# A shorter row of work ahead of the first FFN step, and matmuls on constants in TensorE's idle time there

## The chip, the core and the metric

The kernel runs on one core of a Trainium2 chip. A core has five engines with a queue each, worked off in order: TensorE (PE, matmuls into PSUM), VectorE (DVE), ScalarE (ACT), GpSimd (POOL) and SyncE (SP, which here issues all DMA transfers). They wait for one another by semaphores. The metric is the device time of one execution in microseconds (us).

## What is computed

Windowed attention with global tokens, then a block of a Fourier transform and an FFN, for 8 batches of 544 rows of 512 numbers, all in float32:

```python
s_g  = scale * q_g @ k_all.T;  out_g = softmax(s_g) @ v_all
s_ll = where(|i - j| <= 32, scale * q_l @ k_l.T, -1e9)
s_lg = scale * q_l @ k_g.T
out_l = softmax(concat(s_lg, s_ll)) @ concat(v_g, v_l)
x = concat(out_g, out_l)                    # heads side by side, (8, 544, 512)
mixed = real(fft(fft(x, axis=1), axis=2))
u  = x + mixed
un = (u - mean(u)) / sqrt(var(u) + 1e-6)
out = u + relu(un @ w_ch1) @ w_ch2          # 512 -> 2048 -> 512
```

The weights come as 64-bit numbers. Products in TensorE are made of float16 halves: each operand is split into a high and a low half, and three of the four products are summed (high x high, high x low, low x high).

## The kernel before

**Work and loops.** All work is cut into jobs, a method each of the class `Kern`. A planner (`Plan`, Python that runs when the kernel is built) holds for each job its engine, a cost, what it reads and writes, and a due time; it places them one after another, on each engine the ready job with the earliest due time, and `emit` writes them out in that order. So constants at the head of the file (due times such as `W2_AT`, costs, which tile a step uses) decide the order on every engine. The chip then follows that order, whatever its own durations.

**Stages.** Weights: 32 pieces are loaded (`w_load`), put together from their 64-bit words (`w_low` on POOL or ACT, `w_split64` on ACT into one of two PSUM tiles `ps1`, `w_size` L409 and `w_sign` L423 on DVE), summed on PE (`w_sum` L419), and split: the high half on ACT (`w_hi`), the low half in `w_lo`, on DVE as one instruction (L452), or on POOL as two (L449, L450) for the eight pieces listed in `LOP`. Attention: batch by batch, four pairs of heads each, four units of 128 rows a pair: scores on PE (L604), mask and maximum on DVE (`masked`, L612), exponents and high half on ACT, low half on POOL (`p_lo`, L628), a transposing DMA (`turn`, L633), values on PE (`values`, L649 and L652), division on DVE (`norm`, L663 to L665). Around the rows of the global tokens two rows are swapped by a pair of small DMAs (`x_mid`, L743 and L744). DFT of a batch: even and odd parts on DVE (`d_odd` partly on POOL; `d_even` L812 to L818, `d_even2`, `d_odd2`), halves (`d_hi`, `d_lo` L847), the first DFT on PE (`d_first`, five steps L893 and L895, read out by ACT in `d_z` and DVE in `d_z2` L913), the second DFT (`d_second` L928), added onto the rows by DVE (`d_addc` L954, `d_add` L945); a small rest in `d_tailsec`. FFN: 17 chunks of 256 rows. A chunk has its layer norm on DVE (`l_bn` to `l_v`, then `l_un` L1007, the normalized row in float32, `l_hi` its high half on ACT, `l_lo` L1015 its low half on DVE), a transposing DMA per 128 rows (`l_turn`), and eight times a first step (`f_first` L1047, 24 matmuls of 128x256) and a second step (`f_second` L1066, 12 of 128x512, into the two PSUM tiles `acc0` and `acc1`), with ReLU and halves between them on ACT and DVE (L1052, L1056); at the end DVE reads out the sums (`f_end` L1071).

**Order around the change.** Attention of batch 0 and all weight pieces come first, then the DFT of batch 0, then the layer norm of chunk 0, then the first `f_first`. From there on FFN steps fill PE, and attention and DFT of the next batches are placed between them. PSUM: four general tiles (`bk`, given out as they fall free), two `ps1` and `acc0`, `acc1`. `SPARE` names those PSUM tiles which the DFT of batch 0 may use besides, since no FFN runs yet.

Of the kernel before, what the change touches and what calls it, by code (L numbers as in the profile page):

```python
# [7 lines left out]
F32 = mybir.dt.float32  # L8
F32R = mybir.dt.float32r
F16 = mybir.dt.float16  # L10
# [10 lines left out]
P = 128  # L21
# [9 lines left out]
T0 = 130.0  # L31
STEP = 5.25
PERIOD = 109.0
U_AT, U_PACE = 9.0, 4.0
B_AT, B_PACE = 150.0, 5.0
W_AT, W_PACE = 7.0, 2.6
W2_AT, W2_PACE = 48.0, 2.6
S_AT, S_PACE = 25.0, 4.2
S2_AT, S2_PACE = 190.0, 5.0
B_HOLD = 0.0  # L40
# [1 line left out]
PEF = 1.65  # L42
PEM, PEM0, SPM = 1.5, 0.6, 0.2
LOOK = {"ACT": 0.5, "DVE": 0.5, "POOL": 0.8, "SP": 0.5}
ALOW = 4
LOP = (1, 3, 5, 7, 9, 11, 13, 15)
EARLY = 6
L_HOLD = 50.0
QUEUE = 4.0
LOOK_BY = 30.0  # L50
LN, LN1, LN2 = 50.0, 30.0, 40.0
LNB = True
SPARE = {0: "acc0", 1: "acc1", 4: "ps1", 2: "ps1", (0, 0): "acc0", (0, 1): "acc1"}
BLOCK = (0, 3, 1, 2)


# [65 lines left out]
class Plan:  # L122
# [165 lines left out]
            todo -= 1  # L288

    def emit(self):  # L290
        for j in self.order:
            j.fn(*j.a)


class Kern:
# [524 lines left out]
    def d_even2(self, b):  # L820
# [4 lines left out]
        ve.tensor_add(v(f, 0, 129), c[:, :, 0:129], c[:, :, 256:127:-1])  # L825
        ve.tensor_sub(v(f, 258, 128), c[:, :, 0:128], c[:, :, 256:128:-1])

    def d_odd2(self, b):
        se, s4 = self.nc.vector, self.D[b]["s4"]
        self.odd_rows(se, s4[:, :, P:2 * P])  # L830
        c = s4[:, 2:4, 1:256]
        f = s4[:, 0:2].rearrange("p a d -> p (a d)")
        v = lambda t, o, n: t[:, o:o + 2 * n].rearrange("p (k d) -> p k d", k=2)
        se.tensor_sub(v(f, 0, 128), c[:, :, 0:128], c[:, :, 254:126:-1])
        se.tensor_add(v(f, 256, 128), c[:, :, 0:128], c[:, :, 254:126:-1])
# [166 lines left out]

    def l_un(self, c, j):
        L = self.L[c]
        L["un", j] = un = self.p1.tile([P, DM], F32, name="un", tag="un")
        L["hl", j] = hl = self.p2.tile([P, 2, DM], F16, name="unh")
        self.nc.vector.tensor_scalar(un, self.u_row(c, j), L["ve"][:, 1, j:j + 1], L["ve"][:, 2, j:j + 1], op0=ALU.mult, op1=ALU.add)  # L1007

    def l_hi(self, c, j):
        L = self.L[c]  # L1010
        self.nc.scalar.activation(L["hl", j][:, 0], L["un", j], AF.Copy)

    def l_lo(self, c, j):
        L = self.L[c]
# [70 lines left out]
    def jobs_weights(self, add):  # L1085
# [22 lines left out]
        for m in range(32):  # L1108
            k, t = divmod(m, 16)
            i = t if k else 4 * (t % 4) + t // 4  # L1110
            j = i % 4 * 4 + i // 4 if k == 0 else (i + 16) % 18
            w = (f"w{j}", "w", m)
            h = (f"a{i}" if k == 0 else f"w{(i + 14) % 18}", "h", m)
            self.whobj[k, i] = h
            T = S_AT + S_PACE * m if k == 0 else S2_AT + S2_PACE * t
            ws = ("ws", 0, t // 4) if k == 0 else ("ws", 1, 3)
            add("ACT", .63, self.w_hi, k, i, r=[w, ws], w=[h], t=T)
            if m in LOP:
                add("POOL", 1.95, self.w_lo, k, i, True, r=[w], w=[h], t=T + 1)
            else:  # L1120
                add("DVE", 1.15, self.w_lo, k, i, False, r=[w], w=[h], t=T + 1)

    def jobs_batch(self, add, b):
        gn = ("gn", b)
# [99 lines left out]
            add("POOL", 1.26, self.g_fix, g, r=[("xtg", g), *both("xA")], w=both("xA") + [("xtf", g)], k=[X, xt])  # L1224

    def jobs_dft(self, add, b):
        rate, pem = (PEF, PEM0) if b == 0 else (1.0, PEM)
        accx, dsc, e4, xt, s4, X = ("accx", b), ("dsc", b), ("e4", b), ("xt", b), ("s4", b), ("X", b)
        xtg = [(n, 2 * b + i) for n in ("xtm", "xtf") for i in range(2)]
        add("ACT", .40, self.g_square, b, r=[("xgo", b, 0), ("xgo", b, 1)], w=[accx], k=[("xg", b)])  # L1230
# [8 lines left out]
            add(eng, us, self.d_odd, b, i, r=src, w=[s4h[i]] + ([] if i else [s4]), k=[X, s4])  # L1239
            add("DVE", 3.0 if i else 2.9, self.d_even, b, i, r=src, w=[x4h[i]] + own, k=[X, e4])  # L1240
        add("DVE", 1.35, self.d_even2, b, r=x4h, w=x4h, k=[e4])
        add("DVE", 2.3, self.d_odd2, b, r=s4h, w=s4h, k=[s4], late=6.0)
        et, ht = ("et", b), ("ht", b)
        add("POOL", 3.85, self.d_tail, b, r=xtg, w=[et, ("un", "st", b)], k=[xt])
        eh = [("eh0", b), ("eh1", b)]
# [31 lines left out]
    def jobs_chunk(self, add, c):  # L1277
# [7 lines left out]
            add("DVE", .88, self.l_bn, c, j, r=r0[j:j + 1], w=[("mv", c)], k=[X], t=L, back=LNB)  # L1285
        add("DVE", .80, self.l_v, c, r=[("mv", c)], w=[ve], t=L, back=LNB)
        for j in range(2):
            un, hl = ("un", c, j), ("unh", c, j)
            add("DVE", .58, self.l_un, c, j, r=r0[j:j + 1] + [ve], w=[un, hl], k=[X], t=L, back=LNB)
            add("ACT", .55, self.l_hi, c, j, r=[un], w=[hl], t=L, back=LNB)  # L1290
            add("DVE", .70, self.l_lo, c, j, r=[un, hl], w=[hl], t=L, back=LNB)
            add("SP", 1.3, self.l_turn, c, j, r=[hl], c=[uh], svc=1.6, t=L, margin=SPM, back=LNB)
        add("POOL", 3.0, self.l_root, c, r=[ve, ("ws", 1, 3)], w=[ve], t=T, back=False)
# [21 lines left out]
    def make_plan(self):  # L1315
        one = ["e4", "gn", "xg", "pg", "pgr", "s4", "et", "ht", "eh0", "eh1", "z0", "z1", "zr",
               "un", "lw", "asm", "acc0", "acc1"] + [f"w{i}" for i in range(18)] + [f"a{i}" for i in range(16)]
        rings = dict.fromkeys(one, 1)
        rings.update(qk=3, vf=4, kT=2, qT=2, vN=2, vB=2, gT=2, plg=1, pe=4, ph=3, pl=3, X=3, uh=2, unh=2, ve=4, mv=2, ps1=2,
                     acc=2, accx=2,  dsc=2, z=3, nm=4, ng=2, h=3, ge=2, ra=2, rb=2, es=2, xt=2)  # L1320
        plan = self.plan = Plan(rings, {"bank": 4})
        self.whobj = {}
        add = plan.add
        add("SP", .41, self.msk_load, w=[("msk",)], svc=.7, t=U_AT - 8)
        add("SP", 1.8, self.load_consts, w=[("const",)], svc=2.5, t=U_AT + 20)
        self.jobs_weights(add)
        for b in range(B):
            self.jobs_batch(add, b)
            for p in range(4 * b, 4 * b + 4):
                self.jobs_pair(add, p)  # L1330
            self.jobs_dft(add, b)
        for c in range(17):
            self.jobs_chunk(add, c)
        plan.targets(1.3)
        plan.run()

# [53 lines left out]
```

## Time and profile before

| what | us |
|---|---|
| median of three timed runs | 1033.93 (1028.98 to 1034.74) |
| the profiled execution | 1033.84 |
| its span, first to last instruction | 1032.1 |
| first instruction of the first `f_first` | 146.53 |
| end of the last FFN step | 1022.30 |

The profile is one execution, measured by the chip's profiler. A row of the timeline gives the start, the duration, the engine, the line, the operation, what it writes and reads, and in brackets how long the engine stood idle before it and what ended that. A row of a table by stretches gives the bounds of the stretch, its length, the busy time of each engine with its number of instructions, the clock that TensorE was granted (1.00 is full speed), the busy share of the DMA engines and GB/s. In a list of groups the columns are busy time, mean ns of one, and idle time before them with what ended it; in a list of waits: us in total, times, longest.

### The profile page before, as it was taken

How to read it: one execution, taken by the hardware profiler on the slowest of the kernel's cores; microseconds unless marked ns; L12 is line 12 of the kernel's file. 1: busy time of each engine (PE TensorE's matmuls, PEld its weight loads, DVE VectorE, ACT ScalarE, POOL GpSimd, SP SyncE). 2: the span in 40 equal slices, each digit the busy share in tenths (PEclk: the TensorE clock that was granted, in tenths of full speed). 3: DMA queues.
4: the chain of work that ended last, by engine and by line, in shares of the span. 5: the costliest groups of instructions: out<-in, count | busy, mean ns of one | idle time of the engine just before them, and what ended most of it. 6: DMA issues, size and time to landing. Idle time of an engine off the chain costs nothing. (4 is left out here: it accounts for less than half of the span.)

```text
span 1032.1 us, 25192 instructions
## 1 busy us (share of the span) xinstructions
PE 929.6 (90%) x9864; PEld 651.0 (63%) x9864; DVE 658.1 (64%) x1773; ACT 589.4 (57%) x1291; POOL 531.8 (52%) x797
## 2 busy tenths in 40 slices
PE   2354459999999999999999999999999999999996
PEld 1243347767677767676766676777767676666673
DVE  4887999977768855785598568856775456311111
ACT  7996769973677477637863876487436332111110
POOL 7999756862687278626863774486437302000000
PEclk9985569999999999999999999999999999999998
DMA  9898356462685287328752864466225402102000
GB/s 364 254 269 238 105 107 138 106 140 42 141 130 133 45 160 154 77 55 147 134 131 53 132 155 96 88 117 140 39 55 102 83 1 64 42 1 41 2 21 21
DMA packets 221359, 111.52 MB, mean 108 GB/s; under 512 B 196376, under 2 KB 203704, under 8 KB 221240
## 3 DMA queue, kind: packets, MB, share of 16 engines
q1 hardware_dynamic: 221240, 109.91, 48.5%
q8 instruction: 77, 1.26, 0.5%
q14 instruction: 42, 0.34, 0.1%
HBM read 47.37 MB, written 9.44 MB: 55 GB/s over the span
## 5 line engine op out<-in xcount | busy, mean ns | idle before, releaser
L1047 PE MATMUL ps<-uh,wh 128*128 128x256 f16 x3264 | 379.7, 274 | 0.9 <-DMA uh<-unh 0.9
L1066 PE MATMUL acc<-wh,h 128*128 128x512 f16 x1632 | 375.2, 380 | 1.5 <-DVE h L1056 1.0
L1047 PEld LDWEIGHTS <-wh 128*128 128x128 f16 x3264 | 316.1, 98 | 51.2 <-issue 2.0
L1066 PEld LDWEIGHTS <-h 128*128 128x128 f16 x1632 | 154.3, 98 | 170.3 <-issue 2.5
L1056 DVE SCALAR_TENSOR_TENSOR h<-ps,h 128x512 f16<-128x512 f32 x136 | 93.6, 689 | 236.2 <-ACT h L1052 236.0
L1052 ACT ACTIVATE h<-ps 128x512 f16<-128x512 f32 x136 | 80.7, 593 | 256.4 <-PE ps L1047 255.8
L628 POOL TENSOR_TENSOR ph<-pe,ph 128x448 f16<-128x448 f32 (+1 forms) x128 | 139.4, 1103 | 79.3 <-ACT ph L623 63.3
L612 DVE CUSTOM_DVE_ANT_0 pe<-bk,msk,z 128x224 f32<-128x224 f32 (+1 forms) x256 | 102.4, 454 | 17.4 <-PE bk L604 14.2
L619 ACT ACTIVATE pe<-pe,nm 128x224 f32<-128x224 f32 (+1 forms) x256 | 104.7, 476 | 14.2 <-DVE nm L612 13.9
L1027 POOL TENSOR_TENSOR ve<-ve 128x2 f32<-128x2 f32 x17 | 3.9, 230 | 179.8 <-DVE un L1007 179.8
L649 PE MATMUL bk<-vN,pl 128*128 128x65 f16 x768 | 67.4, 201 | 26.6 <-DMA pl<-ph 17.9
L623 ACT ACTIVATE ph<-pe 128x448 f16<-128x448 f32 (+1 forms) x128 | 71.0, 579 | 22.0 <-DMA pl<-ph 15.2
L649 PEld LDWEIGHTS <-pl 128*128 128x128 f16 x768 | 59.5, 103 | 28.8 <-DMA pl<-ph 23.5
L652 PEld LDWEIGHTS <-pl 96*128 96x128 f16 (+1 forms) x768 | 57.5, 103 | 10.0 <-issue 5.9
L604 PE MATMUL bk<-kT,qT 64*128 64x192 f16 (+2 forms) x1536 | 57.5, 221 | 6.5 <-POOL kT L588 4.2
L604 PEld LDWEIGHTS <-qT 64*128 64x128 f16 x1536 | 50.1, 99 | 20.8 <-issue 16.7
L652 PE MATMUL bk<-vB,pl 96*128 96x65 f16 (+1 forms) x576 | 51.5, 202 | 0.0
L563 POOL TENSOR_TENSOR vN<-vf,vN 128x640 f16<-128x640 f32 x32 | 45.8, 1431 | 6.8 <-ACT vN L559 6.6
L419 PE MATMUL wl<-wm,partb 128*128 128x256 bf16 x64 | 18.8, 398 | 32.0 <-DVE wm L409 32.0
L588 POOL TENSOR_TENSOR kT<-qk,kT 128x559 f16<-128x559 f32 x32 | 40.7, 1271 | 11.8 <-ACT kT L583 11.6
L573 ACT ACTIVATE qk<-qk,z 128x559 f32<-128x559 f32 x64 | 43.7, 729 | 2.1 <-DVE z L514 2.0
L508 ACT ACTIVATE junk<-qk 128x512 f16<-128x512 f32 x64 | 41.3, 645 | 4.4 <-DMA qk<-in_qk 3.4
(170 smaller groups left out, 1350.0 us busy)
## 6 DMA issues: line engine op xcount, KB each, us to landing
qk<-in_qk SPq DMA_DIRECT2D x32, 535.5 KB, 5.2
rw<-in_moe_w_ch SPq DMA_DIRECT2D x22, 512.0 KB, 5.2
vf<-in_v SPq DMA_DIRECT2D x32, 320.0 KB, 3.3
out<-X SPq DMA_DIRECT2D x16, 512.0 KB, 3.1
raw<-in_moe_w_ch SPq DMA_DIRECT2D x10, 512.0 KB
vB<-vN SPq DMA_DIRECT2D x32, 97.5 KB, 2.2
vB<-vN SPq DMA_DIRECT2D x64, 32.5 KB, 2.0
pl<-ph SPq DMA_TRANSPOSE x128, 3.2
```

What stands on the lines that cost most here:

```text
L563: self.nc.gpsimd.tensor_sub(vN[:, :, 1, :, 0:64], self.st[p]["vf"], vN[:, :, 0, :, 0:64])
L604: nc.tensor.matmul(S[h][:, t + w0:t + w1], qT[r, a, j], kT[r, k0:k0 + w1 - w0], start=m == 0, stop=m == 2)
L612: nc.vector.tensor_tensor_reduce(self.per[j][:, h, 0:w], S[h][:, t:t + w], self.msk[:, j, 0:w], z[:, 8:9], 3e38, op0=ALU.add, op1=ALU.min, ...
L619: self.nc.scalar.activation(pe[:, h], pe[:, h], AF.Exp, bias=nm[:, h:h + 1], scale=-1.0)
L623: self.nc.scalar.activation(ph[:, 0, :, 0:WIDE[i % 4]], self.per[i % 4][:, :, 0:WIDE[i % 4]], AF.Copy)
L628: self.nc.gpsimd.tensor_sub(ph[:, 1, :, 0:w], self.per[i % 4][:, :, 0:w], ph[:, 0, :, 0:w])
L649: nc.tensor.matmul(pv[:, j % 2, h], pl[:, 4 * a + 2 * h], vN[:, j, c, h, :], start=m == 0, stop=False)
L652: nc.tensor.matmul(pv[:, j % 2, h], pl[0:n, 4 * a + 2 * h + 1], vb, start=False, stop=m == 2)
L1047: nc.tensor.matmul(ps[:, q], wt[:, w, c0:c0 + P], uh[:, :, 4 * a + kt, :], start=n == 0, stop=n == 11)
L1052: self.nc.scalar.activation(h[:, 0], self.fps[c, fp], AF.Relu)
L1056: self.nc.vector.scalar_tensor_tensor(h[:, 1], self.fps.pop((c, fp)), 0.0, h[:, 0], op0=ALU.max, op1=ALU.subtract)
L1066: nc.tensor.matmul(self.acc_f[c][j], h[:, a, q, j * P:(j + 1) * P], self.w[1, f][:, w, :], start=f == 0 and a == 0 and w == 0, stop=f == 1 ...
```

## The change

It has four parts.

1. Constants of the planner: due times of units and of the second weights, all low halves of weights on DVE (`LOP` empty), cheaper planner costs for two steps, and other PSUM tiles for the DFT of batch 0 (first-DFT steps 0 and 1 now in the two `ps1` tiles).
2. `d_odd2` is split in two jobs, so that the even low half can stand between them.
3. Layer norm: the high half is made by ACT straight from the row (scale and bias of the row as operands) instead of from the float32 row; the second float32 row of a chunk has a buffer of its own (that of `lw`); the high half no longer waits for the float32 row.
4. `warm`: a matmul of 128x512 on two constant tables, into a general PSUM tile that nobody reads. 84 of them are given to the planner, with the lowest urgency and not before planner times 104 and 110; those that it places behind the first `f_first` are not written out, and 56 remain.

```diff
-U_AT, U_PACE = 9.0, 4.0
+U_AT, U_PACE = 4.0, 4.0
-W2_AT, W2_PACE = 48.0, 2.6
+W2_AT, W2_PACE = 40.0, 2.6
-LOP = (1, 3, 5, 7, 9, 11, 13, 15)
-EARLY = 6
+LOP = ()
+EARLY = 4
+WARM = ((14, .45, 104.0), (70, .27, 110.0))
-SPARE = {0: "acc0", 1: "acc1", 4: "ps1", 2: "ps1", (0, 0): "acc0", (0, 1): "acc1"}
+SPARE = {0: "ps1", 1: "ps1", 4: "acc0", (0, 0): "acc0", (0, 1): "acc1"}
...
     def emit(self):
+        t0 = min(j.start for j in self.order if j.fn.__name__ == "f_first")
         for j in self.order:
+            if j.fn.__name__ == "warm" and j.start > t0:
+                continue
             j.fn(*j.a)
...
+    def d_odd1(self, b):
+        self.odd_rows(self.nc.vector, self.D[b]["s4"][:, :, P:2 * P])
     def d_odd2(self, b):
         se, s4 = self.nc.vector, self.D[b]["s4"]
-        self.odd_rows(se, s4[:, :, P:2 * P])
...
     def l_un(self, c, j):
-        L["un", j] = un = self.p1.tile([P, DM], F32, name="un", tag="un")
-        L["hl", j] = hl = self.p2.tile([P, 2, DM], F16, name="unh")
+        L["un", j] = un = self.p1.tile([P, DM], F32, name="un", tag=("un", "lw")[j])
     def l_hi(self, c, j):
-        self.nc.scalar.activation(L["hl", j][:, 0], L["un", j], AF.Copy)
+        L["hl", j] = hl = self.p2.tile([P, 2, DM], F16, name="unh")
+        ve = L["ve"]
+        self.nc.scalar.activation(hl[:, 0], self.u_row(c, j), AF.Identity, scale=ve[:, 1, j:j + 1], bias=ve[:, 2, j:j + 1])
...
-                add("DVE", 1.15, self.w_lo, k, i, False, r=[w], w=[h], t=T + 1)
+                add("DVE", .85, self.w_lo, k, i, False, r=[w], w=[h], t=T + 1)
+    def warm(self, n):
+        self.nc.tensor.matmul(self.bank(("bank", "wm", n)), self.c1[:, 0, 0, 0:P], self.c2.rearrange("p a b c d -> p (a b c d)")[:, 0:512], start=True, stop=True)
+    def jobs_warm(self, add):
+        n = 0
+        for count, us, hold in WARM:
+            for _ in range(count):
+                add("PE", us, self.warm, n, r=[("const",)], w=[("bank", "wm", n)], t=1e6, hold=hold, margin=.1)
+                n += 1
...
-        rate, pem = (PEF, PEM0) if b == 0 else (1.0, PEM)
+        rate, pem = (1.1, PEM0) if b == 0 else (1.0, PEM)
...
-        add("DVE", 2.3, self.d_odd2, b, r=s4h, w=s4h, k=[s4], late=6.0)
+        add("DVE", 1.3, self.d_odd1, b, r=s4h[1:], w=s4h[1:], k=[s4], late=4.0)
+        add("DVE", .95, self.d_odd2, b, r=s4h, w=s4h, k=[s4], late=5.0)
...
-            un, hl = ("un", c, j), ("unh", c, j)
-            add("DVE", .58, self.l_un, c, j, r=r0[j:j + 1] + [ve], w=[un, hl], k=[X], t=L, back=LNB)
-            add("ACT", .55, self.l_hi, c, j, r=[un], w=[hl], t=L, back=LNB)
+            un, hl = (("un", "lw")[j], c, j), ("unh", c, j)
+            add("ACT", .60, self.l_hi, c, j, r=r0[j:j + 1] + [ve], w=[hl], k=[X], t=L, back=LNB)
+            add("DVE", .58, self.l_un, c, j, r=r0[j:j + 1] + [ve], w=[un], k=[X], t=L, back=LNB)
```

The change moves instructions on every engine. Lines shift with it: a line of the kernel before has a number higher by 4 to 7 in the changed kernel (L612 becomes L616, L1007 becomes L1012, L1047 becomes L1054).

**DVE, from the read-out of the first DFT to the layer norm of chunk 0.** L913 (L919 in the change) reads out a first-DFT step, L612 (L616) is half of a masked score unit with its small companion. Before:

```order
L913 SCALAR_TENSOR_TENSOR z_1621<-dps,z_1621 128x2x144
L612 ISA pe_81,nm<-bk_129,msk,z 128x224
L612 ISA nm 128x1
L612 ISA pe_81,nm<-bk_131,msk,z 128x224
L612 ISA nm 128x1
L913 SCALAR_TENSOR_TENSOR z_1621<-dps,z_1621 128x2x144
L913 SCALAR_TENSOR_TENSOR zr<-dps,zr 1x2x144
L913 SCALAR_TENSOR_TENSOR z_1660<-dps,z_1660 128x2x144
L612 ISA pe_82,nm<-bk_130,msk,z 128x224
L612 ISA nm 128x1
L612 ISA pe_82,nm<-bk_128,msk,z 128x224
L612 ISA nm 128x1
```

And the same place now (a row that ends in x2 stands for two like it):

```order
L919 SCALAR_TENSOR_TENSOR z_1595<-dps,z_1595 128x2x144 x2
L919 SCALAR_TENSOR_TENSOR zr<-dps,zr 1x2x144
L919 SCALAR_TENSOR_TENSOR z_1626<-bk_130,z_1626 128x2x144
L919 SCALAR_TENSOR_TENSOR z_1626<-bk_129,z_1626 128x2x144
L616 ISA pe_80,nm<-bk_131,msk,z 128x256
L616 ISA nm 128x1
L616 ISA pe_80,nm<-bk_128,msk,z 128x256
L616 ISA nm 128x1
```

The read-outs now stand in one row, and one masked unit instead of three stands ahead of the second DFT's read-out. A little further on, at the end of the layer norm of chunk 0, before (L517 to L537 are scales of the next pair, L954 the read-out of the second chunk):

```order
L1007 TENSOR_SCALAR un<-X,ve 128x512
L517 TENSOR_SCALAR z<-z 128x2x2
L535 SCALAR_TENSOR_TENSOR z<-z 128x2
L536 TENSOR_SCALAR z<-z,ge 128x2
L537 TENSOR_SCALAR z<-z 128x2x2
L1015 TENSOR_TENSOR unh<-un,unh 128x512
L1007 TENSOR_SCALAR un<-X,ve 128x512
L954 SCALAR_TENSOR_TENSOR X<-bk_129,dsc,X 128x2x128 x4
L1015 TENSOR_TENSOR unh<-un,unh 128x512
```

And now, to the read-out of the second chunk (L960, L951):

```order
L1012 TENSOR_SCALAR un<-X,ve 128x512 x2
L1022 TENSOR_TENSOR unh<-un,unh 128x512 x2
L616 ISA pe_81,nm<-bk_131,msk,z 128x224
L616 ISA nm 128x1
L616 ISA pe_81,nm<-bk_128,msk,z 128x224
L616 ISA nm 128x1
L960 SCALAR_TENSOR_TENSOR X<-bk_130,dsc,X 128x2x128 x4
L951 SCALAR_TENSOR_TENSOR X<-bk_129,dsc,X 128x2x128 x4
```

The four pieces of the layer norm follow one another; the scales and the second chunk's read-out come after them.

**PE, ahead of the first FFN step.** `wh` is a weight's halves, `uh` the transposed halves of the layer norm, `c1r` and `c2r` are constant tables of the DFT. Before, the DFT's tail stands directly ahead of the step:

```order
L928 LDWEIGHTS z_1660
L928 MATMUL bk_131<-c2r,z_1660 32x129
L928 LDWEIGHTS z_1660
L928 MATMUL bk_131<-c2r,z_1660 32x129
L1047 LDWEIGHTS wh
L1047 MATMUL ps_1859<-uh,wh 128x256
```

And now, the last four of 21 fillers (L1131) that stand between the second DFT and the step:

```order
L1131 MATMUL bk_128<-c2r,c1r 128x512
L1131 LDWEIGHTS c1r
L1131 MATMUL bk_130<-c2r,c1r 128x512
L1131 LDWEIGHTS c1r
L1131 MATMUL bk_129<-c2r,c1r 128x512
L1054 LDWEIGHTS wh
L1054 MATMUL ps_1812<-uh,wh 128x256
```

The DFT's tail, the values of units 16 and 17, half of a unit's scores and a small total stand behind the first FFN step now. The other 35 fillers stand ahead of the first DFT or within it (33), and between its second-DFT steps (2). The first of the 21 writes `bk_128`, which one masked unit (17) reads.

**SP, around the row swaps of batch 1.** L743 and L744 (L747 and L748) are the pair of `x_mid`, L633 (L637) the transposes for the values of the next pairs, L567 to L464 loads of the next batch, L1077 (L1084) an output. Before:

```order
L743 DMA X<-xt 1x16x16
L744 DMA xt<-xd 1x16x16
L567 DMA vB_66<-vN 64x780
L568 DMA vB_66<-vN 32x2x260
L569 DMA vB_66<-vN 64x260
L495 DMA vf_68<-in_v 128x640
L464 DMA gn<-in_g 128x256
L633 DMA_TRANSPOSE pl<-ph 128x8x128 x3
```

And now:

```order
L747 DMA X<-xt 1x16x16
L748 DMA xt<-xd 1x16x16
L1084 DMA out<-X 128x2x512
L495 DMA qk<-in_qk 128x1071
L571 DMA vB_66<-vN 64x780
L572 DMA vB_66<-vN 32x2x260
L573 DMA vB_66<-vN 64x260
L499 DMA vf_68<-in_v 128x640
L495 DMA qk<-in_qk 128x1071
L468 DMA gn<-in_g 128x256
```

Four more transfers (the second half of `vB` and `vf_69`) follow there, and only then the transposes: twelve transfers stand between the pair and them, where there were five.

More of the change, by code (lines that the diff above doesn't have):

```diff
@@ L1333, in make_plan @@
             self.jobs_chunk(add, c)
+        self.jobs_warm(add)
         plan.targets(1.3)
```

## The prediction

> **What bounds the kernel now.** The page comes first, then stretches of the run, then the instructions at the ends of those stretches.
>
> ```profile
> span 1032.1 us, 25192 instructions
> PE 929.6 (90%) x9864; PEld 651.0 (63%) x9864; DVE 658.1 (64%) x1773; ACT 589.4 (57%) x1291; POOL 531.8 (52%) x797
> PE   2354459999999999999999999999999999999996
> ```
>
> TensorE (PE) is full from the seventh of 40 slices on. So the time is two things laid end to end: the head before the first FFN step, where PE mostly waits, and the PE work that is left after it. The view of busy time by stretches, cut at the events of the head, says who is busy in each:
>
> ```profile
> core 0: us, PE busy (x) PEld busy (x) DVE busy (x) ACT busy (x) POOL busy (x), PEclk, DMA share, GB/s
> 13.75:110.00 96.25, 45.81 (x595) 30.95 (x595) 77.77 (x208) 83.39 (x177) 87.38 (x97) 0.79 0.95 266
> 110.00:142.50 32.50, 11.68 (x131) 8.85 (x131) 31.54 (x77) 25.76 (x57) 23.71 (x31) 0.61 0.40 97
> 142.50:146.50 4.00, 2.43 (x31) 1.77 (x28) 3.83 (x11) 0.48 (x1) 3.09 (x11) 0.50 0.81 104
> 146.50:152.08 5.58, 5.55 (x30) 3.80 (x32) 4.41 (x13) 2.75 (x6) 2.25 (x6) 0.50 0.30 60
> 152.08:1022.30 870.22, 863.69 (x9087) 605.12 (x9081) 538.65 (x1457) 470.00 (x1036) 407.30 (x635) 1.00 0.44 88
> ```
>
> Row 1 is attention of batch 0 together with the weight preparation: GpSimd (POOL) is busy 87.38 of 96.25 us, the most of any engine, and the DMA engines 0.95. Row 2 is the DFT and layer norm of batch 0: VectorE (DVE) is busy 31.54 of 32.50 us, so the chain there is simply DVE's row of instructions. Row 3 is the last transposing DMA. Row 4 is the first FFN step at clock 0.50. Row 5 is PE alone: 863.69 of 870.22 us. The ends of these stretches, in the timeline:
>
> ```profile
> 111.39 0.68 DVE L812 TENSOR_TENSOR e<-X 128x512 f32<-128x512 f32 x1
> 141.83 0.68 DVE L1015 TENSOR_TENSOR unh<-un,unh 128x512 f16<-128x512 f32 x1
> 146.53 3.79 PE L1047 MATMUL ps<-uh,wh 128*128 128x256 f16 x17 [0.92 <-DMA uh<-unh]
> ```
>
> The second even part of the DFT starts at 111.39, the last low half of the layer norm ends at 142.51 (31.1 us later), and the first FFN step starts at 146.53, released by its DMA. Any move of these three points moves the end by as much, as long as PE stays full behind them.
>
> **Term A, attention of batch 0.** Eight low halves of weights leave POOL for DVE. Instructions of the stretch to 110 us, grouped by line (the last numbers are idle time before them), DVE's first piece there, and whom the DMA queue (SP) waited for with its transposes in 25 to 105 us:
>
> ```profile
> L449 POOL TENSOR_SCALAR wm<-wm,wsc 128x512 f32<-128x512 f32 x8 | 13.4, 1673 | 0.5
> L450 POOL TENSOR_TENSOR wh<-wm,wh 128x512 f16<-128x512 f32 x8 | 9.7, 1210 | 0.7
> L452 DVE SCALAR_TENSOR_TENSOR wh<-wm,wsc,wh 128x512 f16<-128x512 f32 x8 | 6.8, 844 | 0.0
> L409 DVE SCALAR_TENSOR_TENSOR wm<-ps,lw 128x512 int32<-128x512 int32 x32 | 21.8, 686 | 23.6 <-ACT ps L396 17.8 <-POOL lw L405 5.7
> 13.75 0.69 DVE L409 SCALAR_TENSOR_TENSOR wm<-ps,lw 128x512 int32<-128x512 int32 x1 [11.66 <-ACT ps L396]
> SPq L633 <- POOL lw L405: 11.8, 5, 4.4
> SPq L633 <- POOL ph L628: 5.5, 3, 2.9
> ```
>
> POOL loses 13.4 + 9.7 = 23.1 us, DVE gains eight more of the third row, 6.8 us. Two of DVE's weight signs (0.6 us each) also leave the stretch, see B. Then POOL has 64.3 us, ACT 83.4, DVE 77.8 + 6.8 - 1.2 = 83.4. If the new fullest engines reach the occupancy that POOL reached, 87.38 / 96.25 = 0.91, the stretch takes 83.4 / 0.91 = 91.6 us: 4.6 us less. The bounds are 0, because the DMA share of 0.95 leaves no room if transfers are what binds, and -8, about half of SP's 17.3 us of waits for POOL, since a transfer that is issued earlier still meets the same queue. I take **-3.5**: ACT and DVE would both be near the limit, which is worse than one.
>
> **Term B, DFT to layer norm.** DVE is packed here, so the chain changes by what is taken out of its row and put in. Out: two of the three masked score units (L612, four instructions each), the scales of the next pair, and the cosine part of the second chunk (L954, four instructions), all now behind the last low half:
>
> ```profile
> 128.70 0.44 DVE L612 CUSTOM_DVE_ANT_0 pe<-bk,msk,z 128x224 f32<-128x224 f32 x1
> 129.44 0.48 DVE L913 SCALAR_TENSOR_TENSOR z<-dps,z 128x288 f16<-128x288 f32 x1
> 138.30 0.16 DVE L517 TENSOR_SCALAR z<-z 128x4 int32<-128x4 int32 x1
> 139.07 0.69 DVE L1015 TENSOR_TENSOR unh<-un,unh 128x512 f16<-128x512 f32 x1
> 140.26 1.65 DVE L954 SCALAR_TENSOR_TENSOR X<-bk,dsc,X 128x256 f32<-128x256 f32 x4
> 110.79 0.68 DVE L423 SCALAR_TENSOR_TENSOR wm<-ps,wm 128x512 int32<-128x512 int32 x1
> 125.18:128.02 2.84, 2.84 (x22) 2.37 (x23) 2.70 (x10) 2.48 (x8) 1.05 (x1) 0.50 0.28 113
> ```
>
> One masked unit takes 129.44 - 128.70 = 0.74, two 1.5; the scales 139.07 - 138.30 = 0.8; L954 1.65: together 3.95 us out. In: two weight signs (L423, ended at 111.39) that stood ahead of the DFT now stand between its halves, 1.2 us. That is -2.75. What fills the place of the masked units is then a wait: a first-DFT step is 8 matmuls, which at half clock take 2.84 / 22 x 8 = 1.0 us (last row, a stretch of these steps), and the evacuations of the five now follow one another with nothing between. Two steps stand behind the last low half of the DFT; one runs beside the weight maximum, so I charge one, 1.0 us, bounds 0 (full clock) and 2. **-1.7.** The layer norm's new pairing (high half straight from the row on ACT, both float rows on DVE) is not charged apart: DVE's row holds the same four instructions, and ACT's high half runs beside the second float row, 0.55 us.
>
> **Term C, fillers and clock.** After the last DFT matmuls PE is idle, and 21 fillers (128x512) stand directly ahead of the first FFN step. The first of them writes a bank that masked unit 17 reads, and that unit is the DVE piece right behind the last low half, so they start about 0.9 us after it. The price of a filler at full clock is that of an FFN matmul of the same shape, from the chain of waits; the clock comes from half-microsecond stretches:
>
> ```profile
> 1017.09 5.19 PE acc L1066 x24
> 133.71 0.51 PE L928 MATMUL bk<-c2r,z 128*128 128x129 f16 x6 [0.77 <-DVE z L514]
> 125.18 0.30 PE L893 MATMUL dps<-c1r,eh 128*128 128x144 f16 x1 [4.07 <-DVE eh L847]
> 128.00:128.50 0.50, 0.50 (x8) 0.48 (x8) 0.50 (x5) 0.38 (x2) 0.00 (x0) 0.82 0.00 0
> 135.00:135.50 0.50, 0.00 (x0) 0.00 (x0) 0.50 (x2) 0.50 (x2) 0.50 (x1) 0.51 1.17 243
> 152.00:152.50 0.50, 0.50 (x20) 0.49 (x18) 0.02 (x1) 0.45 (x1) 0.36 (x2) 0.92 1.11 215
> ```
>
> 5.19 / 24 = 0.216 us at full clock, so 0.43 at half. The clock rose at 128.18 (0.82 is 0.32 us of full speed in that half microsecond), 3.0 us after PE became busy at 125.18; it fell at 135.0, 0.8 us after PE stopped at 134.2; it rose at 152.08, 5.6 us after 146.53. So a rise takes 3.0 to 5.6 us of work; I take 4.4. In the change PE is idle some 8 us ahead of the fillers, as it is now, so they begin at half clock: 4.4 / 0.43 = 10 at half, 11 at 0.216 = 2.4 us, 6.8 in all, and the first FFN step starts 0.9 + 6.8 = 7.7 us after the last low half, where it is 4.0 now. That costs 3.7. Saved is the first step's half clock, now (152.08 - 146.53) / 2 = 2.8. **+0.9**, bounds -0.5 (rise after 3.0) and +1.7 (after 5.6, and one more wait on a bank). The fillers are therefore not ahead of idle time alone; they end behind the DMA that they cover. The 33 fillers ahead of the first DFT cost nothing: what follows them waits for DVE.
>
> The three clock edges lie 6.82 = 2 x 3.41 and 17.07 = 5 x 3.41 us apart. [...]
>
> **Term D, PE work that moves behind the first FFN step.** One score half, two value steps, the DFT's tail and a small total ran in the head. The last three of these in the head, by a stretch, and a score half at full clock:
>
> ```profile
> 141.90:145.70 3.80, 2.96 (x37) 2.30 (x36) 3.70 (x10) 0.43 (x2) 3.08 (x11) 0.50 1.01 134
> 217.24 0.82 PE L604 MATMUL bk<-kT,qT 64*128 64x192 f16 x24
> 220.63 0.24 PE L649 MATMUL bk<-vN,pl 128*128 128x65 f16 x1 [2.57 <-DMA pl<-ph]
> ```
>
> 2.96 at half clock is 1.5 at full; with 0.8 for the scores **+2.3**. Their cover, PE's idle time, is gone once PE is full, so all of it counts.
>
> **Term E, waits behind the first FFN step.** Row 5 of the stretches has 6.5 us of idle PE. The longest piece is the last row above, 2.57 us for a transposed block, and the clock falls with it:
>
> ```profile
> 209.85 0.69 SPq L743 DMA_DIRECT2D X<-xt  x1
> 212.34 0.51 SPq L744 DMA_DIRECT2D xt<-xd  x1
> 220.00:220.50 0.50, 0.00 (x0) 0.00 (x0) 0.00 (x0) 0.00 (x0) 0.50 (x1) 0.84 1.08 211
> 223.50:224.00 0.50, 0.50 (x3) 0.15 (x2) 0.50 (x1) 0.48 (x1) 0.50 (x2) 0.74 0.22 43
> 1021.09 0.75 DVE L1071 SCALAR_TENSOR_TENSOR X<-acc,ve,X 128x512 f32<-128x512 f32 x1 [2.64 <-PE acc L1066]
> ```
>
> From 220.34 to 223.76 (the 0.84 and the 0.74 of the two clock rows) PE ran at half clock: 1.6 us of its 3.1 busy us there lost, 4.2 us with the wait. The cause stands on SP: the pair of row swaps of batch 1 (L743, then L744, which waits 2.5 us for the first), and behind it, after five loads, the transposes of the next batch. In the change's order twelve transfers stand between the same pair and those transposes, and the value steps they serve come behind later FFN steps. So this wait should go; but only one FFN first step of 2.6 us then stands between the last second step of chunk 0 and the first of chunk 1, and that one waits until two pieces of 0.75 us (last row) have read the sums out, behind whatever DVE has in hand: I charge 1.7. Bounds -4.2 and +1; **-2.5**.
>
> **The sum.** The profiled execution took 1033.84 us (its span and 1.7 around it), the median of the three timed runs is 1033.93, the same for this purpose. 1033.84 - 3.5 - 1.7 + 0.9 + 2.3 - 2.5 = **1029.3 us**.
>
> **Rivals.**
> 1. Transfers bind the attention stretch. For it: DMA share 0.95. Against: SP's 17.3 us of waits for POOL are times in which nothing was issued. A is 0 and the time 1032.8.
> 2. Slower: DVE becomes the bound between 13.75 and 110 us. It has 18.5 us of idle time there; if that idle time consists of waits that remain, the eight low halves lie on the path in full. A is then +6.8 - 1.2 = +5.6 where it was -3.5, and if the wait at 220 also stays, E is 0: 1033.84 + 5.6 - 1.7 + 0.9 + 2.3 = 1040.9. It decides from A = +3.7 on, that is, when 4.9 of the 6.8 us find no idle place. Against it: 12 us of that idle time (23.6 less the 11.66 at the start) stand ahead of the first piece of a weight (L409), and a piece that is ready can fill such a wait.
> 3. All of it works: A at its bound of -8, E -4.2: 1033.84 - 8 - 1.7 + 0.9 + 2.3 - 4.2 = 1023.1. For it speaks that POOL's pieces of 1.7 and 1.2 us stood ahead of the pieces that transposes wait for.
> 4. The fillers do not do what they say: the first FFN step starts at half clock in spite of them, because a wait on a bank breaks their row. C is 3.7 and the time 1032.1.
>
> **How the numbers follow.** The forecast has 0.48, the rivals 0.19, 0.10, 0.15 and 0.08. What a measurement of this kernel can tell from no change is about 0.5%, 5.2 us. The forecast's own spread is some 4 us either way and crosses -5.2 in four of ten cases, which with rival 3 and a little of 1 gives 0.38 for faster; rival 2 gives 0.10 for slower; 0.52 remain. The range runs from 1022.5, just below rival 3, to 1037, halfway between rivals 1 and 2: it leaves out the lower half of rival 3 (0.07) and most of rival 2 (0.08), and a tail of the rest.
>
> **What would show it.** A: the second even part (111.39 now) starts near 108, and POOL is no longer the fullest engine up to there. B: 29.5 us from there to the end of the last low half. C: the first FFN step begins right behind the last filler at clock 1.00, 7 to 8 us after that low half, and its transposed rows had landed before. D: behind that step PE has 0.8 + 1.5 us more work of batch 1 and the DFT's tail. E: no wait of over 2 us between 200 and 240. The prediction is wrong if DVE shows under 5 us of idle time up to the DFT with the DFT no earlier (rival 2), or if the wait for transposed blocks shows up again at another place.

## The result and the profile after

The change makes the kernel slower: **1038.91 us**, median of 20 runs (1034.27 to 1042.08), against 1032.98 us, median of 20 runs (1028.98 to 1035.76), for the kernel before. The ratio is 1.006, with a 95% interval of 1.0049 to 1.0072. That is 5.9 us more where 4.5 us less were forecast, and above the range given.

The profiled execution took 1036.16 us, the second lowest of the 20, so its trace shows a little less of the loss than the median run has. The page of the changed kernel:

```profile
span 1034.2 us, 25279 instructions
PE 938.1 (91%) x9920; PEld 654.0 (63%) x9920; DVE 679.2 (66%) x1781; ACT 595.5 (58%) x1291; POOL 515.6 (50%) x781
PE   2363679999999999999999999999999999999996
```

PE's row is fuller in slices 5 and 6 of the 40, by the fillers; POOL has lost 16 us of work and DVE has gained 21. Busy time by stretches, cut at the same events as before (second even part, last low half of the layer norm, first FFN step, second FFN step), with the stretch up to 110 us ahead for comparison:

```profile
core 0: us, PE busy (x) PEld busy (x) DVE busy (x) ACT busy (x) POOL busy (x), PEclk, DMA share, GB/s
13.75:110.00 96.25, 44.51 (x582) 29.77 (x581) 85.23 (x213) 82.96 (x179) 68.11 (x82) 0.59 0.96 266
112.14:140.63 28.49, 15.93 (x128) 10.09 (x126) 26.76 (x57) 18.85 (x42) 18.21 (x21) 0.80 0.32 87
140.63:147.30 6.67, 5.87 (x21) 2.36 (x21) 6.43 (x21) 2.52 (x6) 3.30 (x13) 0.73 0.88 120
147.30:149.90 2.60, 2.60 (x25) 2.33 (x24) 2.50 (x5) 1.11 (x2) 1.28 (x2) 1.00 0.12 26
149.90:152.70 2.80, 2.80 (x66) 2.41 (x65) 2.04 (x9) 1.21 (x2) 2.00 (x10) 1.00 0.92 175
152.70:1024.50 871.80, 863.70 (x9088) 605.28 (x9087) 552.76 (x1464) 479.83 (x1045) 413.48 (x635) 1.00 0.43 88
```

Row 1: POOL went from 87.38 to 68.11 us, DVE from 77.77 to 85.23, and yet the transfers ran at the same 266 GB/s, with a share of 0.96. The second even part starts at 112.14, not 108. Row 2: 28.5 us to the end of the low half, where the prediction had 29.5. Row 3: the 21 fillers, 5.87 of 6.67 us. Row 4: the first FFN step at full clock. Row 5: 2.8 us of work that stood in the head before. Row 6: as many us of PE work as before (863.7), in 871.8 us instead of 870.22. The waits of PE behind 150 us (us in total, times, longest), and behind them the two long ones as they stand in the timeline:

```profile
PE bk L899 <- DVE nm L616: 4.7, 2, 2.4
PE bk L899 <- DVE eh L853: 1.4, 1, 1.4
PE bk L653 <- DMA pl<-ph: 1.3, 2, 0.7
```

```profile
230.89 0.35 PE L899 MATMUL bk<-c1r,eh 128*128 128x144 f16 x3 [2.31 <-DVE nm L616]
...
645.66 0.22 PE L899 MATMUL bk<-c1r,eh 128*128 128x144 f16 x1 [2.38 <-DVE nm L616]
```

The wait at 220 us is gone. Two new ones stand in its place: the first DFT step of batch 1, and that of batch 5, wait for a PSUM tile that a masked unit on DVE (L616) still reads. Behind the second one the clock fell, as it had behind the wait that went:

```profile
230.50:231.00 0.50, 0.11 (x2) 0.11 (x2) 0.50 (x3) 0.50 (x1) 0.00 (x0) 1.00 0.32 53
646.00:646.50 0.50, 0.50 (x8) 0.50 (x6) 0.50 (x2) 0.50 (x2) 0.06 (x1) 0.50 0.60 174
```

(The third number from the end is the clock: 1.00 beside the first wait, 0.50 behind the second.)

### The profile page after: what moved, and what is told of

It is laid out like the page before. It is cut to its first block, busy times and chain, and to the rows that moved or that the text cites. A ratio compares the mean times of both kernels' runs of the same rounds, so it can differ in the third digit from the quotient of the medians.

```text
span 1034.2 us, 25279 instructions
## 1 busy us (share of the span) xinstructions
PE 938.1 (91%) x9920; PEld 654.0 (63%) x9920; DVE 679.2 (66%) x1781; ACT 595.5 (58%) x1291; POOL 515.6 (50%) x781
## 4 chain that ended last, share of the span: by engine, by line
PE 74%; DVE 13%; DMA 4%; ACT 3%; issue 2%; POOL 2%; SPq 1%; DVEq 0%; POOLq 0%; ACTq 0%
PE ps L1054 31%; PE acc L1073 30%; PE bk L608 3%; PE bk L653 2%; PE bk L656 2%; DMA pl<-ph 2%; PE bk L934 2%; PE bk L899 2%; DVE pe L616 1%; DVE wm L413 1%; PE bk L680 1%; DVE wm L427 1%; DMA vB<-vN 1%; DVE wh L456 1%; DVE eh L853 1%
## 5 line engine op out<-in xcount | busy, mean ns | idle before, releaser
L1054 PE MATMUL ps<-uh,wh 128*128 128x256 f16 x3264 | 378.5, 273 | 0.0
L1054 PEld LDWEIGHTS <-wh 128*128 128x128 f16 x3264 | 315.7, 98 | 51.0 <-issue 0.9
L632 POOL TENSOR_TENSOR ph<-pe,ph 128x448 f16<-128x448 f32 (+1 forms) x128 | 141.7, 1118 | 94.3 <-ACT ph L627 81.1
L616 DVE CUSTOM_DVE_ANT_0 pe<-bk,msk,z 128x224 f32<-128x224 f32 (+1 forms) x256 | 102.4, 454 | 17.8 <-PE bk L608 17.5
L1034 POOL TENSOR_TENSOR ve<-ve 128x2 f32<-128x2 f32 x17 | 12.1, 710 | 158.8 <-DVE unh L1022 107.4
L653 PE MATMUL bk<-vN,pl 128*128 128x65 f16 x768 | 65.7, 200 | 16.7 <-DMA pl<-ph 16.5
L556 POOL TENSOR_TENSOR vf<-vf,z 128x640 f32<-128x640 f32 x32 | 42.0, 1314 | 16.0 <-DVE z L518 11.7
L567 POOL TENSOR_TENSOR vN<-vf,vN 128x640 f16<-128x640 f32 x32 | 45.9, 1437 | 8.2 <-ACT vN L563 4.3
```

Of the source, the lines that this page charges most:

```text
L567: self.nc.gpsimd.tensor_sub(vN[:, :, 1, :, 0:64], self.st[p]["vf"], vN[:, :, 0, :, 0:64])
L616: nc.vector.tensor_tensor_reduce(self.per[j][:, h, 0:w], S[h][:, t:t + w], self.msk[:, j, 0:w], z[:, 8:9], 3e38, op0=ALU.add, op1=ALU.min, ...
L632: self.nc.gpsimd.tensor_sub(ph[:, 1, :, 0:w], self.per[i % 4][:, :, 0:w], ph[:, 0, :, 0:w])
L653: nc.tensor.matmul(pv[:, j % 2, h], pl[:, 4 * a + 2 * h], vN[:, j, c, h, :], start=m == 0, stop=False)
L1054: nc.tensor.matmul(ps[:, q], wt[:, w, c0:c0 + P], uh[:, :, 4 * a + kt, :], start=n == 0, stop=n == 11)
```

## The experiments

Most variants keep an order exactly. The planner first makes its order, jobs are moved in that list, and then the planner is run again with each engine bound to its own part of the list:

```python
v = [(ready(j), j) for j in (cand[e] if seq is None else [j for j in line[e][:1] if need[j.n] == 0])]
```

Jobs that are not moved keep their order on their engine. `new` and `old` are the orders of the change and of the kernel before, each as a head (all jobs that its planner starts before the first FFN step) and a rest. Times are medians, and each is compared with the kernel before in the same set of runs ("over" is the difference of the two medians; the change itself is 5.9 over).

**1. The head of the change with the rest of before.**

```diff
-seq = new.head + new.rest
+seq = new.head + [k for k in old.head + old.rest if k not in new.head]
```

> All jobs that the change puts ahead of the first FFN step stay in its order, fillers included; all others follow in the order of the kernel before. Theory 1 (the new order behind the first FFN step loses more than the head gains): the head is worth 2.1 us (second FFN step 0.6 us later, but with 2.7 us more of other TensorE work done), so about 2 us below the kernel before, 1031, and no wait of 2.3 us for a masked unit at 231 or 646. Theory 2 (the loss is made in the head): no gain over the change, about 1039.

1040.76 us, 9.0 over (1.0089, 1.0056 to 1.0121). At first sight theory 2. But the seam of the two orders made a wait of its own, right behind the head. Timelines of DVE, POOL and PE of this run:

```profile
164.21 5.13 DVE L491 SCALAR_TENSOR_TENSOR wh<-wm,wsc,wh 128x512 f16<-128x512 f32 x1
...
164.34 2.13 POOL L667 TENSOR_TENSOR ph<-pe,ph 128x512 f16<-128x512 f32 x2
166.44 1.23 POOL L627 TENSOR_TENSOR kT<-qk,kT 128x559 f16<-128x559 f32 x1
167.64 1.14 POOL L627 TENSOR_TENSOR qT<-qk,qT 128x512 f16<-128x512 f32 x1
...
170.11 5.28 PE L1089 MATMUL ps<-uh,wh 128*128 128x256 f16 x24 [3.78 <-DVE h L1098]
```

A low half of a weight (L491 in that file) sat on DVE for 5.13 us, an FFN low half queued behind it, PE waited 3.78 us, and the step after it ran 5.28 us, where the first FFN step of this run, at 153.82, takes 2.79 (the first one of the kernel before takes 5.28 too, at a granted clock of 0.50). That is 6.3 us in an execution that took 1043.32 us, 11.6 over. The six runs lie between 1034.80 and 1046.57, and one trace does not say how often this wait comes; so this run says little of the head. The others do.

**2. The head of before with the rest of the change.**

```diff
-seq = new.head + new.rest
+seq = old.head + [k for k in new.head + new.rest if k not in old.head and k[0] != "warm"]
```

> All jobs that the kernel before puts ahead of the first FFN step in its order (low halves of eight weights on POOL, its PSUM tiles, no filler); all others in the order of the change. Theory 1 (new order behind the first FFN step): as slow as the change or 2 us slower, 1039 to 1041. Theory 2 (head): about 1033, as before.

1035.08 us, 3.3 over (1.0034, 1.0018 to 1.0049). Between the two theories: the rest alone costs 3.3 us, and if the parts add, the remaining 2.6 of the 5.9 belong to the head. (The layer norm has the code of the change in this run and in run 8.) PE has the same two waits for a masked unit in this run (L616 is L651 in its file), 4.8 us together:

```profile
PE bk L934 <- DVE nm L651: 4.8, 2, 2.4
```

**3. No fillers.**

```diff
-            if j.fn.__name__ == "warm" and j.start > t0:
+            if j.fn.__name__ == "warm":
```

> The change in its own order, the 56 fillers not written out. If the fillers only trade 2.7 us of later start for 2.8 us of half clock in the first FFN step, as the two traces say: first FFN step at 144.6 at clock 0.50, time within 1 us of the change. Rival (the fillers cost more than that, by banks or by the clock later): 1034 to 1037.

1039.46 us, 7.7 over (1.0077, 1.0053 to 1.01): 1.8 us more than the change in the median, which the intervals can't tell from nothing. The first FFN step in PE's timeline:

```profile
146.40 4.28 PE L1054 MATMUL ps<-uh,wh 128*128 128x256 f16 x24 [10.59 <-DMA uh<-unh]
```

It starts 3.9 us after the last low half (142.49) and takes 4.28 us, where the kernel before has 5.28 in its trace: here the clock rose 3 us into it (it is 0.53 in the half microsecond from 149.00 and 1.00 in the next). Behind the two waits for L616, at 231 and 648 in this run, the clock fell both times (stretches with the clock third from the end):

```profile
232.00:232.50 0.50, 0.50 (x6) 0.50 (x5) 0.50 (x5) 0.50 (x3) 0.00 (x0) 0.50 0.72 276
648.50:649.00 0.50, 0.50 (x6) 0.50 (x5) 0.50 (x2) 0.50 (x2) 0.00 (x0) 0.50 0.80 266
```

**4. Eight low halves on POOL, all orders as in the change.**

```diff
-LOP = ()
+LOP = (1, 3, 5, 7, 9, 11, 13, 15)   # set after the order was made
```

> The change in its own order, the eight low halves on POOL as before (two instructions each). If the relief of POOL is worth nothing because transfers and the chain behind them set the attention stretch: second even part at 112 to 113 as in the change, time within 1 us of it. Rival (the relief did help, something else took it): second even part at 115 or later, 3 us slower than the change, 1042.

1043.75 us, 12.0 over (1.0118, 1.0095 to 1.014), second even part at 118.75. In an order that was made for DVE, POOL cannot have them back. That doesn't say that taking them from POOL helps in the order in which POOL had them; run 6 asks that.

**5. The two waits taken out of the change.**

```diff
+behind(seq, [("d_first", (1, 0)), ("d_first", (1, 1))], ("f_second", (1, 3)))
+behind(seq, [("d_first", (5, 0)), ("d_first", (5, 1))], ("f_first", (9, 1)))
```

> The change in its own order but for two places on PE: the first two first-DFT steps of batch 1 behind the next second FFN step, those of batch 5 behind the next first FFN step (one FFN step later each). Theory 1 (these steps wait for banks that a late DVE still reads, 2.3 us each, and the clock falls with them): both waits go, 4.7 us and up to 3.4 us of half clock, so 1031 to 1034. Rival (DVE is late anyway and the next step waits instead): 1037 to 1039.

1037.2 us, 4.9 over (1.0045, 1.0031 to 1.006). Both waits are gone from the trace and no wait is over 1.4 us (in run 8, which has the same two moves, the clock is 1.00 around both places), but the median is only 1.0 us nearer, less than the intervals can tell.

**6. The kernel before, with nothing changed but the eight low halves on DVE.**

```diff
-LOP = (1, 3, 5, 7, 9, 11, 13, 15)
+LOP = ()   # set after the order was made
```

> The kernel before in its own order on every engine; only the eight low halves stand on DVE instead of POOL (one instruction instead of two). Forecast of the prediction (relief of POOL): second even part at 108, time 3.5 us below the kernel before. Rival 1 (transfers set the stretch): 111 to 112, within 1 us of the kernel before. Rival 2 (DVE becomes the bound): 115 to 117, 4 to 6 us slower.

1032.65 us, 0.3 over (1.0, 0.9985 to 1.0015). Rival 1. The second even part stood at 112.03 instead of 111.39, with POOL relieved by 22 us. The stretch by engines:

```profile
13.75:110.00 96.25, 44.90 (x596) 30.97 (x597) 84.40 (x214) 82.97 (x177) 65.32 (x80) 0.79 0.95 266
```

All engines are below 0.88 of the stretch; the DMA share of 0.95 and the 266 GB/s are those of the kernel before.

**7. Half of the bytes of 26 weight loads, in the order of the change.**

```diff
-        self.nc.sync.dma_start(raw.rearrange("p n t -> p (n t)"), self.w_src(k, i).bitcast(I32))
+        m = 512 if n < 6 else 256
+        self.nc.sync.dma_start(raw[:, 0:m].rearrange("p n t -> p (n t)"), self.w_src(k, i)[:, 0:m].bitcast(I32))
```

> The change in its own order; 26 of the 32 weight loads move half of their bytes (6.8 MB less of 29), and the halves that came are used twice, so the weights are not those of the reference. If transfers set the end of the attention stretch: second even part 4 us earlier or more (108 or before), time less by as much. If DVE's row sets it (full from 25 to 75 us): 112 to 114, time within 1.5 us of the change.

1032.45 us, 0.1 over (1.0002, 0.9988 to 1.0016), so 5.8 less than the change, with the second even part at 108.15. DVE is as full as it was:

```profile
13.75:110.00 96.25, 48.65 (x606) 32.41 (x607) 89.73 (x221) 86.87 (x187) 72.77 (x86) 0.59 0.81 196
25.00:75.00 50.00, 24.86 (x312) 16.81 (x311) 49.32 (x116) 47.53 (x98) 39.05 (x42) 0.53 0.77 178
```

From 25 to 75 us the change has

```profile
25.00:75.00 50.00, 23.82 (x299) 15.37 (x299) 49.31 (x122) 47.26 (x97) 39.16 (x42) 0.57 0.94 266
```

DVE has 49.32 of 50 us here and 49.31 there. The instructions that read the halves of a load twice did not get shorter (ACT's first piece takes 619 ns on average and 618 in the change, POOL's piece 742 and 721), so the bytes are what differs, and with fewer of them the same row of DVE ends earlier.

**8. Run 2 with the two waits taken out** as in run 5.

> The head of the kernel before, the other jobs in the order of the change, with the two first-DFT pairs one FFN step later as in the first run of this set. Theory 1: 5 to 8 us below the same kernel without that (1035.1), so 1027 to 1030, below the kernel before. Rival: no gain, 1035.

1032.08 us, 0.3 under (1.0001, 0.9988 to 1.0014): 3.6 better than run 2. The wait for a masked unit is down to

```profile
PE bk L945 <- DVE nm L662: 0.6, 1, 0.6
```

So the two waits make up the loss of the rest. It had been expected to get below the kernel before, and it doesn't, although the wait at 220 us is gone here too.

**9 to 12. What else is in the head.** In the change the last two weight loads are issued at 99.8 and 101.8 (in the trace of run 5), in the kernel before at 93.5 and 94.1. Run 9 moves them back on SP, run 10 takes two pieces of DVE from ahead of the second even part, run 11 has both and run 5's edit, run 12 has no fillers besides.

```diff
+loads: behind(seq, [("w_load", (1, 14, 30)), ("w_load", (1, 15, 31))], ("w_load", (1, 13, 29)))
+       behind(seq, [("load_v", (5,)), ("load", (6,))], ("turn", (12,)))
+sizes: behind(seq, [("w_size", (1, 14)), ("w_size", (1, 15))], ("d_even", (0, 1)))
```

> The change in its own order but for SP: the last two weight loads ahead of the transposes of units 11 and 12, two loads of the next pairs behind them (as in the kernel before). Theory A2 (the change issues the last weight loads at 99.8 and 101.8, where the kernel before does it at 93.5 and 94.1, and DVE's pieces of these weights hold up the second even part): second even part at 111 to 112 where the traces of the first three variants that keep the change's head have 113.8, 114.5 and 114.9; time 2 to 3 us less than the change, 1036. Rival (the sum of transfers sets it, in any order): 114, 1039.

> The change in its own order but for DVE: the sizes of the last two weights (L413) stand behind the second even part, not ahead of it. Theory A2: second even part at 111.5 to 112.5, 1.2 us less in DVE's row ahead of it and no wait for these weights, time 2 us less, 1037. Rival (the last division waits for its transposed blocks anyway): 113.5 or later, 1039.

> The change with both of these edits and the two first-DFT pairs one FFN step later. If the causes add up: 1038.9 less 2.5 for the second even part and 1.7 to 3 for the two waits, 1033 to 1035, level with the kernel before. If one of them is not a cause: 1036 or more.

> The same three edits, fillers not written out. If the fillers only trade a later start for a faster first step: within 1 us of the run with them. Rival (they hold the first FFN step up by 3 us or more beyond what they save): 3 us less, 1030 to 1031, below the kernel before.

Run 9: 1039.76 us, 7.5 over (1.0074, 1.006 to 1.0089), even part at 114.03, as the rival had it; that the sum of the transfers is the reason is not shown by this run. Run 10: 1040.83, 8.5 over (1.0084, 1.0065 to 1.0103); the even part came to 112.98, but the last low half ended at 143.17, no earlier than elsewhere, since the two pieces now stand behind it. Theory A2 falls with both. Run 11: 1037.77, 5.5 over (1.0057, 1.0041 to 1.0072). Run 12: 1035.52, 3.2 over (1.0027, 1.001 to 1.0043): without fillers 2.3 us less. PE's timelines of runs 11 and 12 at the first FFN step:

```profile
143.34 7.40 PE L1184 MATMUL bk<-c2r,c1r 128*128 128x512 f16 x21 [7.05 <-DVE nm L669]
150.58 2.78 PE L1107 MATMUL ps<-uh,wh 128*128 128x256 f16 x24
155.92 2.25 PE L1107 MATMUL ps<-uh,wh 128*128 128x256 f16 x19
```

```profile
146.35 4.49 PE L1107 MATMUL ps<-uh,wh 128*128 128x256 f16 x24 [10.62 <-DMA uh<-unh]
153.40 4.87 PE L1107 MATMUL ps<-uh,wh 128*128 128x256 f16 x43
```

The last low halves end at 142.54 and 142.41. With fillers the first step begins 4.2 us later and is 1.7 shorter, and the second step begins 2.5 us later.

**13. Moved work back into the idle time**, on top of run 12.

```diff
+ahead(seq, [("scores", (9,)), ("d_tailsec", (0,))], ("f_first", (0, 0)))
```

> The run with three edits and no fillers (1035.5), with one half of a unit's scores and the DFT's tail on PE back ahead of the first FFN step, where PE is idle. Theory (term D: work moved out of the idle time counts in full): 0.8 us of scores and 1.0 of the tail less behind the step, 1033.7. Rival (half clock and the wait for a bank eat it): 1035.5.

1034.27 us, 1.6 over (1.0011, 0.9996 to 1.0027): 1.6 less than run 12, for 1.8 us of work, but the intervals of the two overlap. In the two traces the second step begins at 152.49 and at 153.40, 0.9 apart.

**14. The kernel before, one job on PE later.**

```diff
+behind(seq, [("values", (32,))], ("f_second", (1, 1)))
```

> The kernel before in its own order, but for one job on PE: the values of unit 32, which wait 2.57 us for their transposed block at 220.63, stand behind the next second FFN step. Theory E (that wait and the half clock behind it cost 4.2 us): 1028 to 1030, below both kernels. Rival (the next job waits instead): 1032.

1030.86 us, 1.8 under (0.9977, 0.9959 to 0.9994): better than both kernels. In its trace the clock is 1.00 from 151 to 242 us, and at that place there is only this wait:

```profile
217.55 2.76 PE L1078 MATMUL acc<-wh,h 128*128 128x512 f16 x12
220.52 0.37 PE L455 MATMUL bk<-vax,part 128*128 128x7 f32 x2
221.09 0.20 PE L661 MATMUL bk<-vN,pl 128*128 128x65 f16 x1 [0.21 <-DMA pl<-ph]
```

**15 and 16. The kernel before with half loads**, the low halves on POOL (15) and on DVE (16); the edits are those of runs 7 and 6.

> The kernel before in the order of its planner; 26 of the 32 weight loads move half of their bytes and these are used twice, so the weights are not those of the reference; low halves of eight weights on POOL. Theory (transfers set the attention stretch, POOL would be next): second even part 1 to 3 us earlier than 111.4, 108.5 to 110.5, POOL at 0.90 or more of the stretch. Rival (POOL already binds): 111 to 112, no gain.

> The same with the eight low halves on DVE, the order kept. Theory: with the transfers out of the way the relief of POOL pays what the prediction gave it, 3 to 4 us less than the same kernel with them on POOL. Rival (the relief is worth nothing even then, since DVE takes POOL's place): within 1 us of it.

1030.6 us, 2.1 under (0.9979, 0.9964 to 0.9995), even part at 109.39; and 1026.17, 6.5 under (0.9938, 0.9915 to 0.9961), even part at 105.61. The same stretch of both:

```profile
13.75:110.00 96.25, 45.65 (x598) 31.04 (x598) 79.89 (x213) 85.87 (x184) 88.73 (x99) 0.61 0.78 196
```

```profile
13.75:110.00 96.25, 45.00 (x602) 31.78 (x603) 89.42 (x229) 89.28 (x191) 72.26 (x90) 0.80 0.76 195
```

With the transfers out of the way POOL binds in run 15 (88.73 of 96.25), and its relief is worth 4.4 us. With them in place it is worth nothing (run 6).

## Why the prediction was wrong

The events of the head, from the timelines of the runs with full loads (us; "lag" is from the end of the last low half to the first FFN step):

| head | second even part | end of last low half | lag |
|---|---|---|---|
| before: kernel before, runs 2, 8, 14 | 111.39, 111.61, 111.07, 111.20 | 142.51, 142.82, 142.35, 142.75 | 4.0, 3.7, 4.0, 4.0 |
| change: change, run 5 | 112.14, 114.93 | 140.64, 143.80 | 6.7, 8.2 |
| change, with the moved work ahead of the step: run 1 | 113.80 | 143.74 | 10.1 |
| change without fillers: run 3 | 114.49 | 142.49 | 3.9 |

**Term A (-3.5) is the first step that failed.** The prediction scaled the stretch by the occupancy of its fullest engine; it noted the DMA share of 0.95 and took it for a bound of the gain only. Transfers set the end of the stretch: with half of the bytes of 26 loads the even part came at 109.39 instead of 111.39 in the order of before (run 15) and at 108.15 instead of 112.14 in that of the change (run 7), and the relief of POOL moved it ahead only with these loads (to 105.61 in run 16; 112.03 in run 6). So A is 0 for the low halves themselves: rival 1, given 0.19. In the change the even part is even 2.5 us later (113.8 against 111.3, means of four traces each). Most of that comes with the new order and not with the low halves: with these on DVE in both orders, the order of the change is 1.8 us later with full loads (113.8 against 112.03 in run 6) and 2.5 with half loads (108.15 in run 7 against 105.61 in run 16). Neither the order of the last loads (run 9) nor DVE's pieces ahead of the even part (run 10) account for it; what in the order does stays open. One part of the working was also off: DVE's low halves took 16.5 us for 16 in the change, not 13.6 (its group of instructions to 112 us):

```profile
L456 DVE SCALAR_TENSOR_TENSOR wh<-wm,wsc,wh 128x512 f16<-128x512 f32 x16 | 16.5, 1047 | 0.0
```

**Term B (-1.7) was right in size, and a little more:** 31.3 us before (mean of four) and 28.8 in the change (mean of four), -2.5. Together with A that is 0: the last low half ends at 142.6 before and at 142.7 in the change (means; the four traces of the change lie between 140.64 and 143.80), where -5.2 was forecast.

**Term C (+0.9) had the mechanism right and one of its two sizes wrong.** The fillers do hold the clock (the first FFN step ran at 1.00 in the change, and in run 3 at 0.50 for its first 3 us), and they end behind the transfer that they cover. The lag with them was 6.7 to 8.2 us in seven traces, for 7.7 forecast, and 3.9 without. What they save was mis-sized: 2.8 us were taken from the one trace of before, where the first step takes 5.28 us; it takes 4.68 in run 14, with the same head. In runs 3, 12 and 13 it took 4.2 to 4.5 us without fillers, and 2.78 with, so 1.4 to 1.7 are saved. That makes +2.3, which is what runs 11 and 12 give, where the two waits for L616 are taken out. In the order of the change itself it does not show: run 3, without fillers, is not faster than the change. Why the two pairs of runs differ stays open. The spread of the lag is the clock's: the 21 fillers took 6.0 us in the change and 7.6 in run 5. The clock rose at 144.18 in the change and at 150.49 in run 5 (by the granted clock of half-microsecond stretches, 0.82 from 144.00 and 0.51 from 150.00), 2.8 and 5.9 us after the first of them. What sets the moment of the rise was not shown.

**Term D (+2.3) fits what was measured:** the stretch of moved work has 2.80 us, and moving 1.8 of it back gave 1.6 in the median, which is not clear of noise, and 0.9 in the traces (run 13).

**Term E (-2.5) failed as a forecast of the sum.** The wait at 220 went, as the prediction said. It is worth 1.8 us in the median (run 14), not 4.2. But the new order has two waits elsewhere, for a PSUM tile instead of a transposed block: +3.3 (run 2), which is gone without them (run 8). Since the 1.8 of the wait at 220 should be in run 8 as a gain, some 1.5 us seem to be lost at other places; where is open. The prediction allowed for a wait between chunks 0 and 1 that did not come, and did not read the new order of PE against that of DVE further on, where DVE is 2.3 us late for two first-DFT steps. Its own sign, no wait of over 2 us between 200 and 240, failed at 230.89 (2.31 us). The clock falls behind such a wait in some executions only: of the two waits of a trace, it fell behind one in the change and in run 10, behind both in runs 3 and 7 and behind none in run 9, so behind 6 of 10.

**The sum with what was measured:** A and B +0.1, C +2.3, D +2.8, E +3.3 make +8.5, where +5.9 was measured. The terms come from different sets of runs, each uncertain by 1 to 2 us, and run 5 gained 1.0 from an edit that gained 3.6 in run 8, so part of E seems not to add to the rest, and C does not show in the order of the change (run 3). That 2.6 us is not settled. The slower rival's time (1040.9) is near the measured one, but its reason is not: the low halves on DVE cost 0.3 us (run 6), and DVE kept 11.0 us of idle time up to 110 us (96.25 less 85.23), where the rival's sign was under 5.

## What to carry to other kernels

Where the transfer queues are full in a stretch (here a DMA share of 0.95), test that first (halve the bytes, keep the order) before any engine is relieved: the same relief gave nothing with full loads and 4.4 us with half of their bytes. When a planner makes a new order, look for the waits of the bounding engine at all places of the new order, not only at the one that is meant to go; one job moved by hand (run 14) did more than the whole change. A filler that ends later than the transfer it covers has to earn back that delay (here the first step began 6.7 to 8.2 us behind the last low half instead of 3.9, and was 1.4 to 1.7 us shorter), and the idle time it fills could have taken real work (run 13).

## What the runs showed of the hardware

The same DVE instruction, the low half of a weight with two inputs in SBUF, took 5.13 us in run 1 at 164.21, and 0.74 us at 171.78 in the same run. In the first case POOL had four instructions back to back, from 164.34 to 168.78, and DVE's instruction ended at 169.34, right behind them; up to 171 us no further one of POOL follows. In the change the 16 low halves of weights on DVE took 0.74 to 1.81 us up to 112 us, and the sizes of weights, one input of which is in PSUM, 684 ns on average, with POOL busy for 68.11 of 96.25 us there (group of DVE instructions to 112 us):

```profile
L413 DVE SCALAR_TENSOR_TENSOR wm<-ps,lw 128x512 int32<-128x512 int32 x32 | 21.6, 684 | 16.0 <-ACT ps L400 15.9
```

That POOL's four instructions held DVE's up is a reading of this one place. Elsewhere it is less plain: in the kernel before, DVE's low half (L452) at 43.26 took 0.74 us in the middle of one of POOL's (L449, 42.33 to 43.89), and the one at 23.88 took 1.12 us beside two others (L588).
